# Two feed-forward layers behind a linear attention on one Trainium2 core: the first pass's weight split moves from GpSimd to ScalarE and VectorE, and each chunk's products with low parts come last

## The chip, the cores and the metric

One core of one Trainium2 chip. The metric is the device time of one execution in microseconds; for the kernel before it was measured in three runs. A separate execution was recorded by the hardware profiler and is the source of every row below. Engines are named as in the profile: PE is TensorE (PEld its weight loads), DVE is VectorE, ACT is ScalarE, POOL is GpSimd, SP is SyncE, which here only issues DMAs.

## The reference

```python
def _attn_ref(q, k, v):            # (4, 8, 576, 64) each
    q_s = softmax over the last axis of q
    k_s = softmax over the sequence axis of k
    kv = np.einsum('bhsd,bhse->bhde', k_s, v)
    return np.einsum('bhsd,bhde->bhse', q_s, kv)

x = attn_out.transpose(0, 2, 1, 3).reshape(2304, 512)
h = x @ w_in1; x = (h * sigmoid(h)) @ w_out1         # SiLU,  512 -> 2048 -> 512
h = x @ w_in2; x = (h * tanh(softplus(h))) @ w_out2  # Mish,  512 -> 2048 -> 512
```

The softmaxes subtract the maximum and divide by the sum plus 1e-9. The feed-forward weights reach the chip as 64-bit floating point numbers and are turned into fp32 on the chip; q, k and v are fp32.

## The kernel before, in words

**Layers and passes.** The 2304 tokens are six blocks of 384 (`BLK`, index `j`). Each feed-forward layer is cut into 16 chunks of 128 hidden columns (index `c`) and done in two passes of eight chunks, so that the weights of one pass stay in SBUF: pass 0 and 1 are the SiLU layer, pass 2 and 3 the Mish layer. In a pass, every block goes through eight chunks. `ev_g1` (L645) makes the first products of a chunk (hidden values into a PSUM bank `h`, then SiLU or Mish on ACT into `gf`, then a split of `gf` on DVE), and `ev_g2` (L662) the second products, which add the chunk to the block's four (layer 1) or three (layer 2) accumulators in PSUM; it runs three chunks behind (`SKEW`). `ev_e` (L683) evicts the accumulators. In layer 1 the hidden values have two PSUM banks, so the first product of chunk 5 waits until ACT has read chunk 3.

**Split products.** fp32 operands are split into a high part (fp32r, rounded by a copy) and a low part (the difference), and a product is the sum of three matmuls: high by high, high weight by low activation, low weight by high activation. A chunk has 12 first products (four slices of 128 input features, `kc`, by three parts), and 12 second products in layer 1 or 9 in layer 2. Blocks are split by `ev_x` (L635) on ACT and DVE into `xs`. Weights are split as they arrive: a DMA brings a staging tile `st`; ACT makes `wt` from the upper words (`ACTIVATE wt<-st`), DVE shifts the lower words (`TENSOR_SCALAR st<-st`) and joins the two (`SCALAR_TENSOR_TENSOR wt<-wt,st`). For the 16 weight tiles of pass 0, `w_late` (L168) then lets POOL make the high part (`TENSOR_SCALAR w<-wt`) and the low part (`TENSOR_TENSOR w<-wt,w`). The 48 tiles of the later passes are split by `w_high` and `w_low` (L257, L262), on ACT and DVE.

**Attention under pass 0.** Block 0's attention is written out as a list of steps (`START`, L88); that of blocks 1 to 5 (`attn_steps`) is dealt out between the chunks of pass 0. For a pair of heads (index `hp`, 0 to 3) the steps are: turn k on PE, maximum on DVE, Exp on ACT, turn back on PE, copy by ACT ("ke copy"), 12 products k by v on PE ("kv", rows `psum<-xb,xa 64x64`), scaling on DVE (`kvf`); and for q: maximum on DVE (`qmx`), subtraction on POOL, Exp on ACT, sum on DVE (`qz`), normalisation on POOL (`qn`), turn on PE, copy by ACT (`qT`), product with `kvf` on PE, copy by ACT into the block. Block 1 needs the k of a new batch for all four pairs; its chunks can't start their products with slice `kc` before pair `hp = kc` is done. For block 3 the maximum of k is taken along the free axis (`kmx`, 96x768) without a turn.

**What sets the order.** Every engine runs its queue in order. Until the attention is done, a scheduler sets the order on each engine by priorities; a changed instruction can so move others. After that (`InOrder.on`, from pass 1 on), each engine runs in the order of the program text. SP issues all loads and waits, in its queue's order, until the place a load writes is free.

The nine matmuls of `ev_g1` and `ev_g2` and the two instructions of `w_late` are what the change touches.

Of the kernel before, what the change touches and what calls it, by code (L numbers as in the profile page):

```python
# [7 lines left out]
F32 = mybir.dt.float32  # L8
# [3 lines left out]
ALU = mybir.AluOpType  # L12
# [43 lines left out]
def attention_silu_mish(ctx: ExitStack, tc: tile.TileContext, q, k, v, w_in1, w_out1, w_in2, w_out2, out):  # L56
    nc = tc.nc
    SP = nc.sync
    V, S, G, T = (InOrder(tc, e) for e in (nc.vector, nc.scalar, nc.gpsimd, nc.tensor))
# [4 lines left out]
    P = 128  # L64
    NP = H // 2
    KC = DM // P
# [5 lines left out]
    BLK = 384  # L72
# [42 lines left out]
    def banks(name, ids, n=1):  # L115
        i = turns[name] = (turns.get(name, -1) + 1) % len(ids)
        return psum[:, ids[i] * 512:(ids[i] + n) * 512]
# [50 lines left out]
    def w_late():  # L168
        if state["late"] is None:
            return  # L170
        t, w = state["late"]
        state["late"] = None
        tf = t.bitcast(F32)
        G.tensor_scalar(out=w[:, 0], in0=tf, scalar1=1.0, scalar2=0.0, op0=ALU.mult, op1=ALU.add)
        G.tensor_tensor(out=w[:, 1], in0=tf, in1=w[:, 0].bitcast(F32), op=ALU.subtract)

    def w_decode():

        kind, p, _, c = need[state["dec"]]
        now = tc.cur_priority  # L180
        at(nat[need[state["dec"]]] - W_LEAD)
        state["dec"] += 1
        if not st_q:
            w_dma()
        st = st_q.pop(0).rearrange("p (n t) -> p t n", t=2)
        lo, hi = st[:, 0], st[:, 1]
        t = pools["tm"].tile([P, 512], U32, tag="wt", name="wt")
        V.tensor_scalar(out=lo, in0=lo, scalar1=29, scalar2=None, op0=ALU.logical_shift_right)
        S.activation(out=t.bitcast(F32), in_=hi.bitcast(F32), func=ACTF.Prelu, scale=W_BIAS, alpha=W_SIGN)
        w_late()  # L190
        V.scalar_tensor_tensor(out=t, in0=t, scalar=3, in1=lo, op0=ALU.logical_shift_left, op1=ALU.bitwise_or)
        w = wres.tile([P, 2, 512], F32R, tag="wi" if kind == "G1" else "wo", name="w")
        state["late"] = (t, w)
        w_late()
        wt[(kind, p, c)] = w
        if state["dma"] < N0:
            w_dma()
        tc.cur_priority = now
# [9 lines left out]
    def w_get(kind, p, c):  # L208
        while p == 0 and (kind, p, c) not in wt:
            w_decode()  # L210
        return wt[(kind, p, c)]
# [421 lines left out]
    xs, acc, gt = {}, {}, {}  # L633
# [11 lines left out]
    def ev_g1(p, j, c):  # L645
        L = passes[p][0]
        w = w_get("G1", p, c)
        x = xs[(p, j)]
        h = banks("h1", (4, 5) if L == 0 else (4, 5, 6, 7))[:, :BLK]
        for kc in range(KC):  # L650
            wh, wl = w[:, 0, kc * P:(kc + 1) * P], w[:, 1, kc * P:(kc + 1) * P]
            T.matmul(h, wh, x[:, kc, 0], start=(kc == 0), stop=False)
            T.matmul(h, wh, x[:, kc, 1], start=False, stop=False)
            T.matmul(h, wl, x[:, kc, 0], start=False, stop=(kc == KC - 1))
        g = gr.tile([P, 2, BLK], F32R, tag="g", name="g")
        gf = gp.tile([P, BLK], F32, tag="gf", name="gf")
        S.activation(out=gf, in_=h, func=ACTF.Silu if L == 0 else ACTF.Mish)
        V.tensor_copy(g[:, 0], gf)
        V.tensor_tensor(out=g[:, 1], in0=gf, in1=g[:, 0].bitcast(F32), op=ALU.subtract)
        gt[(p, j, c)] = g  # L660

    def ev_g2(p, j, c, tiles=None):  # L662
        L, c0, c1 = passes[p]
        w = w_get("G2", p, c)
        g = gt[(p, j, c)]
        if c == c0:
            acc[(p, j)] = [banks("acc", (0, 1, 2, 3)) for _ in range(KC if L == 0 else NT2)]
        st, sp = (c == c0), (c == c1 - 1)
        for i, a in enumerate(acc[(p, j)]):
            if tiles is not None and i not in tiles:  # L670
                continue
            s = slice(i * P, (i + 1) * P)
            if L == 0:
                o = a[:, :BLK]
                T.matmul(o, w[:, 0, s], g[:, 0], start=st, stop=False)
                T.matmul(o, w[:, 0, s], g[:, 1], start=False, stop=False)
                T.matmul(o, w[:, 1, s], g[:, 0], start=False, stop=sp)
            else:
                T.matmul(a, g[:, 0, s], w[:, 0], start=st, stop=False)
                T.matmul(a, g[:, 0, s], w[:, 1], start=False, stop=False)  # L680
                T.matmul(a, g[:, 1, s], w[:, 0], start=False, stop=sp)

    def ev_e(p, j, tiles=None):  # L683
        L, c0, c1 = passes[p]
# [25 lines left out]
        out=ident, in_=ident, compare_op=ALU.not_equal, fill=1.0, base=0, pattern=[[-1, P]], channel_multiplier=1  # L710
# [23 lines left out]
    steps = {"first": 0, "rest": 0}  # L734
# [12 lines left out]
    for i, (what, p, j, c) in enumerate(events):  # L747
        if "xs" not in pools and state["dec"] == N0 and not order and i >= xat[1] + PACE[1] * steps["rest"] + A_END:
            w_late()
            l1.close()  # L750
            for nm, nb in (("st", 3), ("tm", W_WAIT), ("xs", 1)):
                pools[nm] = ctx.enter_context(tc.tile_pool(name="l" + nm, bufs=nb, reuse_waits="tile"))
            w_plan(i + 0.5)
            InOrder.on = True
# [15 lines left out]
        if i >= len(events) - SKEW - 2:  # L770
            if what == "G2":
                tail.append(c)
                continue
            for n in range(NT2):
                for c in tail:
                    ev_g2(p, j, c, (n,))
                ev_e(p, j, (n,))
            continue
        if what == "E":
            at(i if InOrder.on else i - X_LEAD)  # L780
            ev_e(p, j)
            continue
        (ev_g1 if what == "G1" else ev_g2)(p, j, c)
        w_ahead(1.0)
        if p == 0 and order:
# [33 lines left out]
```

## Time and profile before

| | |
|---|---|
| median of three runs | 898.5 us (895.59 to 898.77) |
| the profiled execution's own time | 900.18 us |
| its span, first to last instruction | 898.4 us |
| around the span | 1.8 us |
| PE busy | 875.8 us (97%), 5002 matmuls and as many weight loads |
| DVE busy | 452.5 us (50%) |
| ACT busy | 297.3 us (33%) |
| POOL busy | 86.8 us (10%) |
| mean granted TensorE clock | 0.991 |

Busy shares are means over stages that differ. The windows view cuts the span into stretches and gives for each the busy time of every engine, the granted clock and the share of the DMA engines; a stretch with PE below its length, or with the clock below 1.00, is where time can be lost. 1.00 is the higher of the clock's two levels (2.4 GHz), 0.50 the lower (1.2 GHz). Matmuls overlap, so the duration of one is longer than the distance from one to the next.

### The profile page before, as it was taken

The page shows a single profiled execution, that of the slowest core. Times are in us where ns is not written, and L with a number is a line of the kernel's source. Part 1 is how long each engine was busy: PE and PEld are TensorE (multiplying, and loading weights), DVE is VectorE, ACT ScalarE, POOL GpSimd, SP SyncE. Part 2 cuts the span into 40 slices and gives each one's busy share as a digit, 9 for nine tenths or more (in the row PEclk, how much of TensorE's full clock was granted, in tenths as well). Part 3 has the DMA queues.
Part 4 walks back from the last instruction along what each step waited for, and adds up shares of the span by engine and source line. Part 5 has one row for each costly group of instructions (what it writes and reads, how often), then busy time and mean ns, then how long its engine had stood idle before and what let it go on. Part 6 is the DMA issues. An engine that isn't in the chain of part 4 may idle for free.

```text
span 898.4 us, 12437 instructions
## 1 busy us (share of the span) xinstructions
PE 875.8 (97%) x5002; PEld 816.8 (91%) x5002; DVE 452.5 (50%) x949; ACT 297.3 (33%) x576; POOL 86.8 (10%) x114
## 2 busy tenths in 40 slices
PE   7888999999999999999999999999999999999998
PEld 6678888899999999999999998998998998998997
DVE  4997656674257644442348444542349533333332
ACT  5665345554245422121135222222235311211210
POOL 3975302121000000000000000000000000000000
PEclk9998999999999999999999999999999999999999
DMA  9992601220023502200004202200003000000000
GB/s 232 227 242 60 143 13 46 49 62 10 1 94 120 162 24 71 71 24 1 1 1 128 61 24 71 71 24 1 1 1 117 1 36 33 3 36 36 1 36 35
DMA packets 61914, 53.23 MB, mean 59 GB/s; under 512 B 30368, under 2 KB 55456, under 8 KB 61856
## 3 DMA queue, kind: packets, MB, share of 16 engines
q1 hardware_dynamic: 61856, 52.44, 20.7%
q8 instruction: 39, 0.64, 0.3%
q14 instruction: 19, 0.16, 0.1%
HBM read 47.71 MB, written 4.72 MB: 58 GB/s over the span
## 4 chain that ended last, share of the span: by engine, by line
PE 88%; DVE 6%; DMA 2%; SPq 1%; ACT 1%; issue 1%; POOL 0%; ACTq 0%; DVEq 0%; POOLq 0%
PE psum L49 72%; PE psum L47 16%; DVE g L47 1%; DMA st<-in_moe_w_in_dram 1%; DVE wt L47 1%; DVE kmx L47 1%; DVE st L47 1%; SPq L319 1%; DVE xs L47 0%; DMA xb<-in_k_dram 0%; DVE qz L47 0%; DVE qmx L47 0%; ACT xa L47 0%; DMA xa<-in_q_dram 0%; SPq L345 0%
## 5 line engine op out<-in xcount | busy, mean ns | idle before, releaser
L49 PE MATMUL psum<-xs,w 128*128 128x384 f32 x1836 | 335.6, 335 | 1.3 <-DVE xs L49 0.8
L49 PEld LDWEIGHTS psum<-xs,w 128*128 128x128 f32 x1836 | 322.0, 188 | 7.0 <-DVE xs L49 1.1
L49 ACT ACTIVATE gf<-psum 128x384 f32<-128x384 f32 x153 | 75.0, 491 | 405.8 <-PE psum L49 322.3
L49 PE MATMUL psum<-w,g 128*128 128x512 f32 x864 | 208.0, 392 | 0.0
L49 PEld LDWEIGHTS psum<-w,g 128*128 128x128 f32 x864 | 161.3, 188 | 31.0
L49 DVE CAST g<-gf 128x384 fp32r<-128x384 f32 x153 | 55.0, 360 | 253.7 <-ACT gf L49 253.7
L49 PE MATMUL psum<-g,w 128*128 128x384 f32 x720 | 130.6, 334 | 0.0
L49 PEld LDWEIGHTS psum<-g,w 128*128 128x128 f32 x720 | 125.3, 188 | 0.0
L47 PE MATMUL psum<-xs,w 128*128 128x384 f32 x468 | 100.1, 353 | 2.7 <-ACT gf L47 2.3
L49 DVE TENSOR_TENSOR g<-gf,g 128x384 fp32r<-128x384 f32 x153 | 85.4, 558 | 5.3
L47 PE MATMUL psum<-g,w 128*128 128x384 f32 x432 | 87.3, 349 | 0.4 <-DVE g L47 0.4
L47 PEld LDWEIGHTS psum<-xs,w 128*128 128x128 f32 x468 | 81.2, 191 | 6.7 <-POOL w L47 2.3
L47 PEld LDWEIGHTS psum<-g,w 128*128 128x128 f32 x432 | 77.0, 193 | 1.8 <-DVE g L47 0.9
L47 DVE CAST g<-gf 128x384 fp32r<-128x384 f32 x39 | 16.8, 431 | 39.6 <-ACT gf L47 39.4
L49 ACT CAST w<-wt 128x512 fp32r<-128x512 f32 x48 | 29.6, 618 | 21.0 <-DVE wt L49 17.8
L49 DVE TENSOR_TENSOR w<-wt,w 128x512 fp32r<-128x512 f32 x48 | 32.6, 686 | 0.6 <-ACT w L49 0.4
L47 ACT ACTIVATE gf<-psum 128x384 f32<-128x384 f32 x39 | 18.8, 491 | 40.9 <-PE psum L47 35.4
L49 ACT ACTIVATE wt<-st 128x512 f32<-128x512 f32 x48 | 31.8, 672 | 0.0
L47 ACT ACT_TABLE_LOAD x22 | 28.2, 1283 | 3.4 <-PE psum L47 2.3
L49 DVE TENSOR_TENSOR xa<-psum,xa 128x512 f32<-128x512 f32 x18 | 12.3, 692 | 31.9 <-PE psum L49 31.9
L47 DVE TENSOR_TENSOR g<-gf,g 128x384 fp32r<-128x384 f32 x39 | 27.8, 713 | 1.1
L47 ACT COPY xa<-psum 128x384 f32<-128x384 f32 (+2 forms) x36 | 19.4, 538 | 23.4 <-PE psum L47 22.3
(108 smaller groups left out, 588.7 us busy)
## 6 DMA issues: line engine op xcount, KB each, us to landing
st<-in_moe_w_in_dram SPq DMA_DIRECT2D x32, 512.0 KB, 3.9
st<-in_moe_w_out_dram SPq DMA_DIRECT2D x32, 512.0 KB, 3.4
out_dram<-xa SPq DMA_DIRECT2D x18, 256.0 KB, 2.0
xb<-in_k_dram SPq DMA_DIRECT2D x16, 144.0 KB, 3.4
xb<-in_v_dram SPq DMA_DIRECT2D x8, 288.0 KB, 6.6
xa<-in_k_dram SPq DMA_DIRECT2D x16, 144.0 KB, 5.7
xb<-in_v_dram SPq DMA_DIRECT2D x16, 144.0 KB, 3.5
qt<-in_q_dram SPq DMA_DIRECT2D x8, 192.0 KB, 2.7
```

The costliest lines, as they stand in the source:

```text
L47: return call(*args, **kwargs)
L49: self.last = call(*args, **kwargs)
L319: SP.dma_start(kt[:, :, h, :], k[b, 2 * hp + h].rearrange("(p r) d -> p r d", r=KR))
```

## The change

`w_late` puts the high part of a pass 0 weight on ACT and the low part on DVE; POOL has no part in the weights any more. `ev_g1` issues the four slices high by high, then the four with the low activation, then the four with the low weight; the first two chunks of block 0 keep the old order. `ev_g2` does the same over its accumulators, so that each matmul goes to another PSUM bank than the one before, where three in a row went to one.

```diff
@@ w_late
-        G.tensor_scalar(out=w[:, 0], in0=tf, scalar1=1.0, scalar2=0.0, op0=ALU.mult, op1=ALU.add)
-        G.tensor_tensor(out=w[:, 1], in0=tf, in1=w[:, 0].bitcast(F32), op=ALU.subtract)
+        S.copy(w[:, 0], tf)
+        V.tensor_tensor(out=w[:, 1], in0=tf, in1=w[:, 0].bitcast(F32), op=ALU.subtract)
@@ ev_g1
-        for kc in range(KC):
-            wh, wl = w[:, 0, kc * P:(kc + 1) * P], w[:, 1, kc * P:(kc + 1) * P]
-            T.matmul(h, wh, x[:, kc, 0], start=(kc == 0), stop=False)
-            T.matmul(h, wh, x[:, kc, 1], start=False, stop=False)
-            T.matmul(h, wl, x[:, kc, 0], start=False, stop=(kc == KC - 1))
+
+        steps = [(kc, i) for i in range(3) for kc in range(KC)]
+        if (p, j) == (0, 0) and c < 2:
+            steps.sort()
+        for n, (kc, i) in enumerate(steps):
+            s = slice(kc * P, (kc + 1) * P)
+            T.matmul(h, w[:, i // 2, s], x[:, kc, i % 2], start=(n == 0), stop=(n == len(steps) - 1))
@@ ev_g2
-        for i, a in enumerate(acc[(p, j)]):
...
-                T.matmul(o, w[:, 0, s], g[:, 0], start=st, stop=False)
-                T.matmul(o, w[:, 0, s], g[:, 1], start=False, stop=False)
-                T.matmul(o, w[:, 1, s], g[:, 0], start=False, stop=sp)
...
+        for n, (iw, ig) in enumerate(((0, 0), (0, 1), (1, 0))):
+            for i, a in enumerate(acc[(p, j)]):
...
+                if L == 0:
+                    T.matmul(a[:, :BLK], w[:, iw, s], g[:, ig], start=st and n == 0, stop=sp and n == 2)
+                else:
+                    T.matmul(a, g[:, ig, s], w[:, iw], start=st and n == 0, stop=sp and n == 2)
```

The scheduler gives pass 0 another order on every engine up to about the fourth chunk of block 1; behind that PE's instructions stand in the same order as before. Three places follow, the rows before and then the rows of the change.

ACT, block 0: the SiLU of chunk 2 (`gf_518`) to that of chunk 3 (`gf_583`). `xb,kz` is the Exp of a k pair, `xb<-xb` those of q, `xa` the ke copy, `wt` the first step of a weight, ACT_TABLE_LOAD the change between Exp and SiLU.

```order
L47 ACTIVATE gf_518<-psum_78 128x384
L47 ACT_TABLE_LOAD
L47 ACTIVATE xb_77,kz_404<-psum_78,knm_402 128x576
L47 ACTIVATE wt_835<-st_775 128x512
L47 ACT_TABLE_LOAD
L47 ACTIVATE gf_583<-psum_78 128x384
```

```order
L47 ACT_TABLE_LOAD
L47 ACTIVATE xb_77,kz_423<-psum_78,knm_421 128x576
L47 ACTIVATE xb_77<-xb_77 96x256 x3
L47 CAST w_839<-wt_835 128x512
L47 ACTIVATE xb_77<-xb_77 96x256
L47 COPY xa_76<-psum_78 96x768
L47 ACTIVATE wt_869<-st_842 128x512
L47 ACTIVATE wt_904<-st_876 128x512
L47 ACTIVATE wt_957<-st_911 128x512
L47 CAST w_873<-wt_869 128x512
L47 ACT_TABLE_LOAD
L47 ACTIVATE gf_583<-psum_78 128x384
```

Between the SiLU of chunk 0 and that of chunk 3 there now stand six new CASTs (two of them here), three more `wt`, two more table loads, the second k pair's Exp, the four Exps of q and the ke copy, which all came after it before.

SP, the loads behind the last weights of pass 0: `xa<-in_q` is the q of block 2 for one pair (here pair 2), `xa<-in_k` half of the k of block 3 for one pair (here pair 1).

```order
L319 DMA xa<-in_k_dram 96x6x64 x2
L345 DMA xa<-in_q_dram 128x2x192
L345 DMA qt<-in_q_dram 128x2x192
L331 DMA xb<-in_v_dram 96x6x64 x2
L319 DMA xa<-in_k_dram 96x6x64
```

```order
L319 DMA xa<-in_k_dram 96x6x64
L345 DMA xa<-in_q_dram 128x2x192
L319 DMA xa<-in_k_dram 96x6x64
L345 DMA qt<-in_q_dram 128x2x192
L331 DMA xb<-in_v_dram 96x6x64 x2
```

The q load writes where pair 2's k lies until its kv is done; the second half of pair 1's k now stands behind it.

DVE, the end of block 1's attention, up to the scaling `kvf` of pair 3 (`kmx` is the maximum of block 3's k for pairs 0 and 1, `xb<-psum` an eviction of block 0, `xs` a low part of block 1).

```order
L47 TENSOR_REDUCE kmx<-xa 96x128
L47 TENSOR_TENSOR xs<-xa,xs 128x384
L47 COPY xb<-psum 128x384
L47 TENSOR_REDUCE qmx<-xa 128x6
L47 SCALAR_TENSOR_TENSOR kvf<-psum,krz,mask 128x128
```

```order
L47 TENSOR_REDUCE qmx<-xa 128x6
L47 TENSOR_REDUCE kmx<-xa 96x128 x2
L47 TENSOR_REDUCE qz<-xa 128x6 x2
L47 TENSOR_SCALAR qz<-qz 128x6
L47 TENSOR_TENSOR xs<-xa,xs 128x384
L47 COPY xb<-psum 128x384 x2
L47 RECIPROCAL qrz<-qz 128x6
L47 TENSOR_SCALAR qz<-qz 128x6
L47 TENSOR_REDUCE qz<-xa 128x6
L47 SCALAR_TENSOR_TENSOR kvf<-psum,krz,mask 128x128
```

Before, the first of the two `kmx` stood ahead of pair 2's `kvf`; now both stand behind it and behind the `qmx` of pair 2's q, and ahead of pair 3's `kvf`.

## Rows read from the trace of the kernel before

**Rows 1.** Windows; columns: stretch, length, PE, PEld, DVE, ACT, POOL busy, clock, DMA share, GB/s.

```profile
20.00:60.00 40.00, 35.16 (x263) 29.45 (x264) 37.87 (x69) 29.13 (x50) 32.55 (x33) 0.96 0.95 239
60.00:100.00 40.00, 33.26 (x205) 29.80 (x205) 31.89 (x67) 21.92 (x44) 23.72 (x31) 0.83 0.49 111
100.00:898.00 798.00, 791.88 (x4406) 743.78 (x4404) 373.26 (x790) 236.59 (x464) 23.62 (x36) 1.00 0.14 44
```

**Rows 2.** Waits of PE, 30 to 104 us; columns: total us, times, longest.

```profile
PE psum L47 <- DVE kvf L47: 3.3, 1, 3.3
PE psum L47 <- POOL qn L47: 2.7, 1, 2.7
```

**Rows 3.** Windows of 5 us behind these two waits.

```profile
65.00:70.00 5.00, 5.00 (x20) 4.81 (x20) 3.67 (x5) 2.43 (x4) 3.47 (x4) 0.51 0.90 166
85.00:90.00 5.00, 5.00 (x21) 4.62 (x19) 2.56 (x7) 1.99 (x6) 2.81 (x4) 0.50 0.33 69
```

**Rows 4.** DVE's groups, 20 to 100 us; columns: count, busy us, mean ns, idle before.

```profile
L47 DVE SCALAR_TENSOR_TENSOR wt<-wt,st 128x512 uint32<-128x512 uint32 x16 | 16.9, 1054 | 1.3 <-DVE st L47 0.5 <-ACT wt L47 0.3
L47 DVE TENSOR_SCALAR st<-st 128x512 uint32<-128x512 uint32 x15 | 10.7, 716 | 1.2 <-DMA st<-in_moe_w_in_dram 1.2
L47 DVE TENSOR_TENSOR g<-gf,g 128x384 fp32r<-128x384 f32 x8 | 8.7, 1093 | 0.2
...
L47 DVE TENSOR_REDUCE kmx<-xa 96x128 f32<-96x768 f32 x2 | 3.1, 1526 | 0.0
```

**Rows 5.** The same work on DVE, 100 to 898 us, mostly without POOL.

```profile
L49 DVE TENSOR_TENSOR g<-gf,g 128x384 fp32r<-128x384 f32 x153 | 85.4, 558 | 5.3
...
L49 DVE TENSOR_TENSOR w<-wt,w 128x512 fp32r<-128x512 f32 x48 | 32.6, 686 | 0.6 <-ACT w L49 0.4
...
L49 DVE SCALAR_TENSOR_TENSOR wt<-wt,st 128x512 uint32<-128x512 uint32 x31 | 21.3, 686 | 0.6
...
L49 DVE TENSOR_SCALAR st<-st 128x512 uint32<-128x512 uint32 x31 | 13.1, 423 | 0.0
```

**Rows 6.** POOL's weight work in pass 0, 20 to 100 us.

```profile
L47 POOL TENSOR_TENSOR w<-wt,w 128x512 fp32r<-128x512 f32 x16 | 22.8, 1426 | 1.1
L47 POOL TENSOR_SCALAR w<-wt 128x512 fp32r<-128x512 f32 x16 | 12.7, 795 | 10.5 <-DVE wt L47 8.1 <-DVE qz L49 2.5
```

**Rows 7.** The high part on ACT, later passes (costliest groups of the page).

```profile
L49 ACT CAST w<-wt 128x512 fp32r<-128x512 f32 x48 | 29.6, 618 | 21.0 <-DVE wt L49 17.8
```

**Rows 8.** ACT's groups, 20 to 100 us.

```profile
L47 ACT ACT_TABLE_LOAD x9 | 11.5, 1283 | 0.2
L47 ACT ACTIVATE wt<-st 128x512 f32<-128x512 f32 x16 | 10.7, 677 | 5.0 <-POOL w L47 2.6 <-DMA st<-in_moe_w_in_dram 2.3
...
L47 ACT COPY xa<-psum 96x768 f32<-96x768 f32 x4 | 3.1, 788 | 1.0 <-DMA xb<-in_q_dram 0.6 <-PE psum L47 0.3
...
L47 ACT ACTIVATE xb<-xb 96x256 f32<-96x256 f32 x8 | 2.9, 407 | 0.6 <-POOL xb L47 0.6
```

**Rows 9.** ACT's timeline, SiLU of chunks 2 and 3; columns: start, us, what, idle before.

```profile
39.74 0.49 ACT L47 ACTIVATE gf<-psum 128x384 f32<-128x384 f32 x1 [2.17 <-PE psum L47]
...
42.50 0.74 ACT L47 ACTIVATE xb<-psum,knm 128x576 f32<-128x576 f32 x1 [0.96 <-DVE knm L47]
...
45.22 0.49 ACT L47 ACTIVATE gf<-psum 128x384 f32<-128x384 f32 x1
```

**Rows 10.** PE's timeline: the 97th chunk product, pair 1's kv, later chunks.

```profile
53.61 1.72 PE L47 MATMUL psum<-g,w 128*128 128x384 f32 x9
...
58.98 0.92 PE L47 MATMUL psum<-xb,xa 96*64 96x64 f32 x24
...
107.53 2.24 PE L47 MATMUL psum<-g,w 128*128 128x384 f32 x12
109.61 2.24 PE L47 MATMUL psum<-xs,w 128*128 128x384 f32 x12
```

**Rows 11.** Loads of k (L319), 55 to 130 us: landing after issue.

```profile
DMA to landing us min/median/max: 3.3/4.5/6.8
```

More of the change, by code (lines that the diff above doesn't have):

```diff
@@ L668, in ev_g2 @@
         st, sp = (c == c0), (c == c1 - 1)
-        for i, a in enumerate(acc[(p, j)]):
[L670 to L674, printed above, removed]
-                T.matmul(o, w[:, 0, s], g[:, 0], start=st, stop=False)
-                T.matmul(o, w[:, 0, s], g[:, 1], start=False, stop=False)
-                T.matmul(o, w[:, 1, s], g[:, 0], start=False, stop=sp)
[L678 to L681, printed above, removed]
+        for n, (iw, ig) in enumerate(((0, 0), (0, 1), (1, 0))):
+            for i, a in enumerate(acc[(p, j)]):
+                if tiles is not None and i not in tiles:
+                    continue
+                s = slice(i * P, (i + 1) * P)
+                if L == 0:
+                    T.matmul(a[:, :BLK], w[:, iw, s], g[:, ig], start=st and n == 0, stop=sp and n == 2)
+                else:
+                    T.matmul(a, g[:, ig, s], w[:, iw], start=st and n == 0, stop=sp and n == 2)
     def ev_e(p, j, tiles=None):
```

## The prediction

> **What bounds the kernel now.** I read the windows first. From 100 us on PE is busy 791.88 of 798 us at clock 1.00, so that stretch is PE's own work; from 20 to 100 us PE is idle 4.8 and 6.7 us, and the clock is 0.96 and 0.83 [rows 1]. Only this stretch, which is pass 0 on block 0 with the attention of block 1, has time to give. In 20 to 60 us DVE is busy 37.87 of 40 us, ACT 29.13, POOL 32.55 [rows 1]: DVE's queue sets the pace there.
>
> PE's waits come next. Two are long, 3.3 us for DVE's `kvf` of pair 1 and 2.7 us for POOL's `qn` of pair 2 [rows 2], and behind each the clock falls to its lower level, 0.51 and 0.50 in the windows that follow [rows 3]. There PE is busy, but at half rate: 5.00 x 0.49 = 2.45 us and 5.00 x 0.50 = 2.5 us lost. The two waits with their clock cost 3.3 + 2.45 + 2.7 + 2.5 = 10.95 us.
>
> Last the groups, to see why DVE is late. The same DVE instruction takes 1054, 716 and 1093 ns beside POOL, and 686, 423 and 558 ns without it [rows 4, 5]. POOL's weight work and DVE slow each other.
>
> **From 100 us on: nothing, 0.** The number of matmuls and their shapes are unchanged, and PE's queue stands in the same order. The product order is another one, but a run of 12 that stays in one bank and a run that changes bank take the same 2.08 us, from 107.53 to 109.61 us, so 0.174 us a product [rows 10]; evicting four accumulators at the end of a chunk has four chunks of first products as cover. If that cover is gone, each chunk start waits for some evictions; I see no reason for it. A gain made before 100 us is passed on whole.
>
> **DVE and POOL in pass 0.** Removed from POOL: 22.8 + 12.7 = 35.5 us of its 32.55 + 23.72 = 56.3 us between 20 and 100 us, 63% [rows 1, 6]. Relief on DVE, if all slowing goes: 16 x 0.368 = 5.9, 15 x 0.293 = 4.4, 8 x 0.535 = 4.3, in all 14.6 us [rows 4, 5]; if it goes by POOL's share, 63%, 9.2 us. Added to DVE: 16 low parts at 0.686, 11.0 us [rows 5]. Net on DVE between -3.6 and +1.8 us: its sum hardly falls. What changes is that DVE no longer stands still in 1 to 2 us pieces, and that `kvf` and `qz` come sooner in its queue. The Trainium skill, "SBUF — State Buffer", section "Who interferes with whom", says that DVE and GpSimd share a port pair under an exclusive lock, held for a whole instruction, and that a DVE instruction with two SBUF inputs takes part in it; by that the 16 new low parts would hold up POOL's remaining q work in turn, up to 11 us in all, and the waits for `qn` would stay. That is one way into the second rival below.
>
> **ACT in pass 0.** Added: 16 high parts at 0.618 = 9.9 us [rows 7], most of them before 60 us, where ACT has 10.9 us idle [rows 1]. ACT becomes as full as DVE is now. What is queued behind them is the SiLU of chunks. Between those of chunk 0 and chunk 3 the order puts six CASTs (3.7), three `wt` (2.0), two table loads (2.6) [rows 7, 8], one Exp (0.74) [rows 9], four small Exps (half of 2.9) and a copy (0.8) [rows 8] more: 11.3 us. The two waits now there, 2.17 and 0.96 us [rows 9], are covered by the fuller queue. So the SiLU of chunk 3 starts not at 45.22 but at 45.2 + 11.3 - 3.1 = 53.4 us and ends at 53.9. The first product of chunk 5 waits for it. The change has laid 60 first and 36 second products ahead of that; the trace has done 96 by 53.61 us [rows 10]. So PE stands at 53.9 where it stood at 53.6: the lateness is paid for by the second products done earlier. From there the same products and the same attention lead to the end of pair 1's kv, 59.9 us now [rows 10]. **Up to there: 0**, bounds -3.6 (DVE's net) and +8.2 (the whole delay of that SiLU).
>
> **The first wait (kvf of pair 1).** In the changed DVE queue `kvf` stands right behind a low part whose CAST follows the ke copy on ACT; both run while PE makes kv, 0.92 us [rows 10]. `kvf` can then follow kv at once, and PE has three products and two turns as cover. I leave 0.5 us and take away 3.3 + 2.45.
>
> **The second wait (qn of pair 2).** A `kmx` of 1.526 us [rows 4] stood ahead of the `qz` that POOL needs; it now stands after. I leave 0.5 us and take away 2.7 + 2.5.
>
> **A new wait (kvf of pair 3).** SP's order puts half of pair 1's k behind the q load that must wait for pair 2's kv, and DVE's queue holds the `qmx` of that q and both `kmx` ahead of pair 3's `kvf`. After pair 2's kv: landing 4.5 us [rows 11], seven DVE rows of 384 columns at 0.56 (3.9) and two `kmx` (3.05) [rows 4, 5], 11.5 us. PE has meanwhile 32 chunk products at 0.174 (5.6) and some 3.4 us of attention, 9.0. I take +2.5 us. With the landing at 3.3 or 6.8 us [rows 11] it would be 1.3 or 4.8; it is 0 if ACT holds PE up there anyway, and if the clock falls behind it, 2.5 us more.
>
> **Block 1's first chunk.** Slice 3 is now the fourth product of 12, not the tenth, so PE has 13 products less to do while ACT copies and rounds pair 3's part: bounds 0 and 13 x 0.174 = 2.3 us. Two turns and a product of block 2 stand there too; I take +1.0.
>
> **The sum.** -10.95 + 0.5 + 0.5 + 0 + 2.5 + 1.0 = -6.45 us. Against the profiled execution 900.18 - 6.5 = 893.7 us. The median of the three runs, 898.5, lies 1.7 us below it, so I predict 892.0 us.
>
> **Rivals.**
>
> *Slower: ACT takes DVE's place.* ACT's queue is in order, and three `wt` in a row now stand ahead of chunk 3's SiLU, two ahead of the next ke copy; if one of their weights lands late, ACT stands still and PE behind it. Should that hold PE twice for as long as now, 10.95 us, the gain is gone and the rest stays: 0.5 + 0.5 + 2.5 + 1.0 = 4.5 us, 903.0 us. It decides once the SiLU of chunk 3 starts some 3 us after 53.4. For it: DMA share 0.95 in 20 to 60 us [rows 1]. Against it: ACT waited only 2.3 us for weights [rows 8]. Chance 0.14.
>
> *No change: one hold stays.* POOL's q work is still slowed, or DVE is still behind, and one of the two waits with its clock (5.45 us) stays: 892.0 + 5.45, about 897.5 us. For it: DVE's sum hardly falls. Chance 0.21.
>
> *More: PE alone.* All 10.95 us go and DVE's net of 3.6 shows too, with no new wait: 898.5 - 14.6 = 883.9 us. Against it: five engines' queues would have to fit. Chance 0.10.
>
> *The rotation of banks costs clock.* If changing the bank at every second product let the clock fall there, half of the 798 us would take twice as long, some 1,300 us. A run that changes bank every third product shows neither a gap nor a clock below 1.00 today [rows 1, 10]. The Trainium skill, "TensorE: Matmul & The Clock Gate", section "A second HAM failure mode: psum-queue depth-cycling", reports a kernel in which cycling through PSUM banks did make the clock oscillate; this trace does not bear it out at three products a bank. Chance 0.02.
>
> **How the numbers follow.** The forecast has 0.53. 0.5% is 4.5 us, about what a measurement of this kernel can tell from no change. Faster by more than that (below 894.0): the PE case whole, and 0.48 of the forecast's 0.53, 0.58. Slower (above 903.0): half of the ACT case and the banks, rounded up, 0.10. The rest, 0.32. The range runs from 885, a little above the PE case, to 902, which takes in the no-change case and part of the ACT case; some 0.06 lies below it and 0.10 above.
>
> **What would show it.** Right: no `w` rows on POOL; `wt<-wt,st` near 700 to 850 ns in pass 0; 16 more CASTs of about 0.62 us on ACT; no wait of PE for `kvf` of pair 1 or `qn` of pair 2 above 1 us and the clock at 1.00 from 60 to 80 us; a wait for pair 3's `kvf` of 1 to 5 us; the same time per product after block 1. Wrong: a wait of PE for `gf` of chunk 3 or for a ke copy of more than 3 us with a fall of the clock behind it; or any difference that arises after 100 us.

## The result: 8 us faster, and the profile after

The changed kernel took 888.2 us, the median of six executions (887.8 to 892.2); the kernel before, on the same chip, 896.3 us, the median of six (895.6 to 898.8). The ratio is 0.9911, 95% interval 0.9889 to 0.9933: 8.1 us less. The profiled execution took 888.09 us, its span 886.3; that of before, 900.18 us, lies above all six of before's executions here, so the two traces differ by 12.1 us, more than the medians. The section on the prediction comes back to that.

The windows of the changed kernel that answer to [rows 1] and [rows 3], with the same columns:

```profile
20.00:60.00 40.00, 35.01 (x269) 28.95 (x269) 38.29 (x88) 35.21 (x64) 10.73 (x13) 1.00 1.04 255
60.00:100.00 40.00, 38.79 (x265) 35.47 (x266) 31.06 (x72) 24.81 (x50) 15.06 (x20) 1.00 0.66 142
100.00:886.00 786.00, 780.64 (x4339) 732.16 (x4337) 365.60 (x779) 233.00 (x459) 21.34 (x32) 1.00 0.14 42
...
65.00:70.00 5.00, 5.00 (x36) 4.81 (x35) 4.03 (x10) 3.71 (x11) 0.00 (x0) 1.00 0.39 70
85.00:90.00 5.00, 5.00 (x30) 4.86 (x29) 4.85 (x10) 3.67 (x6) 3.58 (x5) 1.00 1.15 239
```

PE does 38.8 us of work in 60 to 100 us where it did 33.3, and all at the full clock. POOL's busy time in 20 to 60 us is a third of what it was, ACT's is up by 6.1 us, and DVE's is as full as before: 38.3 of 40 us. All waits of PE from 30 to 104 us (us in total, times, longest):

```profile
PE psum L47 <- ACT gf L47: 1.9, 2, 1.2
PE psum L47 <- DVE g L47: 1.2, 1, 1.2
PE psum L47 <- ACT qT L47: 0.8, 2, 0.6
PE psum L47 <- DVE kvf L47: 0.7, 1, 0.7
PE psum L47 <- ACT xs L49: 0.3, 1, 0.3
PE psum L47 <- ACT xa L47: 0.3, 1, 0.3
```

The waits for `kvf` of pair 1 and `qn` of pair 2 [rows 2] are gone, and no wait is longer than 1.2 us. DVE's groups from 20 to 100 us, to be read beside [rows 4]:

```profile
L47 DVE SCALAR_TENSOR_TENSOR wt<-wt,st 128x512 uint32<-128x512 uint32 x16 | 11.0, 692 | 0.1
L47 DVE TENSOR_TENSOR w<-wt,w 128x512 fp32r<-128x512 f32 x16 | 10.7, 681 | 0.7 <-ACT w L47 0.6
L47 DVE TENSOR_TENSOR g<-gf,g 128x384 fp32r<-128x384 f32 x13 | 9.2, 710 | 0.3
L47 DVE TENSOR_SCALAR st<-st 128x512 uint32<-128x512 uint32 x15 | 7.0, 475 | 0.4 <-DMA st<-in_moe_w_in_dram 0.4
```

The join of the halves takes 692 ns where it took 1054, the low part of `g` 710 for 1093, the shift 475 for 716. The 16 new low parts fill what this set free. Where the time went is read from PE's timeline. The start of pair 1's kv, of a kv further on and of the last run of pass 3, in the kernel before:

```profile
58.98 0.92 PE L47 MATMUL psum<-xb,xa 96*64 96x64 f32 x24
...
130.66 0.92 PE L47 MATMUL psum<-xb,xa 96*64 96x65 f32 x24
...
886.27 8.36 PE L49 MATMUL psum<-w,g 128*128 128x512 f32 x36
```

and in the changed kernel:

```profile
57.19 0.92 PE L47 MATMUL psum<-xb,xa 96*64 96x64 f32 x24
...
119.03 0.92 PE L47 MATMUL psum<-xb,xa 96*64 96x65 f32 x24
...
874.20 8.36 PE L49 MATMUL psum<-w,g 128*128 128x512 f32 x36
```

The lead is 1.8 us at 58 us, 11.6 us at 131 and 12.1 at 886 (it is 12.1 already at 270, where a run of 12 starts at 270.33 before and at 258.26 after). Most of it, 9.8 us, arises between 59 and 131 us; from there it is carried along but for 0.5 us.

### The profile page after: what moved, and what is told of

Its sections match the earlier page's. It is cut to its first block, busy times and chain, and to the rows that moved or that the text cites. A ratio compares the mean times of both kernels' runs of the same rounds, so it can differ in the third digit from the quotient of the medians.

```text
span 886.3 us, 12434 instructions
## 1 busy us (share of the span) xinstructions
PE 869.8 (98%) x5002; PEld 810.4 (91%) x5002; DVE 444.6 (50%) x965; ACT 303.1 (34%) x592; POOL 54.0 (6%) x82
## 4 chain that ended last, share of the span: by engine, by line
PE 72%; DVE 0%; ACT 0%; issue 0%
PE psum L49 72%; DVE xa L49 0%; ACT xs L49 0%
## 5 line engine op out<-in xcount | busy, mean ns | idle before, releaser
L49 PE MATMUL psum<-g,w 128*128 128x384 f32 x720 | 130.6, 334 | 0.0
L49 PEld LDWEIGHTS psum<-g,w 128*128 128x128 f32 x720 | 125.3, 188 | 0.0
L49 DVE TENSOR_TENSOR g<-gf,g 128x384 fp32r<-128x384 f32 x153 | 85.5, 559 | 5.3
L47 PE MATMUL psum<-g,w 128*128 128x384 f32 x432 | 84.8, 343 | 1.2 <-DVE g L47 1.2
L47 PEld LDWEIGHTS psum<-g,w 128*128 128x128 f32 x432 | 74.7, 188 | 2.6 <-DVE g L47 1.7
L47 DVE CAST g<-gf 128x384 fp32r<-128x384 f32 x39 | 16.3, 419 | 38.8 <-ACT gf L47 38.5
L49 DVE TENSOR_TENSOR xb<-psum,xb 128x384 f32<-128x384 f32 x24 | 11.7, 550 | 30.6 <-PE psum L49 30.6
L47 DVE TENSOR_TENSOR g<-gf,g 128x384 fp32r<-128x384 f32 x39 | 25.0, 641 | 1.0
```

What stands on the lines that cost most here:

```text
L47: return call(*args, **kwargs)
L49: self.last = call(*args, **kwargs)
```

## The experiments

The change has two parts, where the weights are split and the order of the products. My theory was that the first pays, because DVE and POOL hold each other up when they work side by side. The rivals were that the order pays, that what pays is only that POOL's queue is short, or that it is ACT taking over the copies. Every ratio is against the kernel before on the same chip, whose median was 896.9 us (17 executions) for the first four runs, 897.7 (7) for the next three and 897.4 (19) for the last three. A difference from the changed kernel's 888.2 us is one between chips, on which the kernel before lay up to 1.4 us apart; where it matters the ratios are given beside it.

**The split alone (e1_split).** `ev_g1` and `ev_g2` as before, `w_late` as in the change:

```diff
@@ ev_g1, from the changed kernel
-        steps = [(kc, i) for i in range(3) for kc in range(KC)]
...
+        for kc in range(KC):
+            wh, wl = w[:, 0, kc * P:(kc + 1) * P], w[:, 1, kc * P:(kc + 1) * P]
...
```

> Only the weight split moves to ScalarE and VectorE; the products keep their old order (high-high, high-low, low-high slice by slice, three in a row per bank). Theory A (moving the split is what pays): 887 to 890 us, 6.5 to 9 below the kernel before, PE's waits for kvf of pair 1 and qn of pair 2 are below 1 us and the clock stays at 1.00 from 60 to 100 us. Theory B (putting the low parts last is what pays, because PE no longer waits for them): 896 to 900 us, with new waits of PE for the low parts that VectorE now makes, 3 us or more in all between 30 and 60 us.

Measured 888.6 us (888.0 to 891.2), ratio 0.9909 [0.9895, 0.9924]: the whole gain. Its longest waits of PE are those of the changed kernel, 1.4 us and less.

**The order alone (e2_order).** The new order of products, the weights on POOL as before:

```diff
@@ w_late, from the changed kernel
-        S.copy(w[:, 0], tf)
-        V.tensor_tensor(out=w[:, 1], in0=tf, in1=w[:, 0].bitcast(F32), op=ALU.subtract)
+        G.tensor_scalar(out=w[:, 0], in0=tf, scalar1=1.0, scalar2=0.0, op0=ALU.mult, op1=ALU.add)
+        G.tensor_tensor(out=w[:, 1], in0=tf, in1=w[:, 0].bitcast(F32), op=ALU.subtract)
```

> Only the products change their order; GpSimd keeps splitting pass 0's weights. Theory A: 895 to 897 us, within 1.5 us of the kernel before; VectorE's join of weights still takes about 1050 ns on average in pass 0 and PE still waits 2 us or more for kvf of pair 1 or for qn of pair 2. Theory B: 887 to 890 us.

Measured 896.4 us (894.7 to 898.2, 12 executions), ratio 0.9992 [0.9981, 1.0003]: no difference that can be told. PE's waits, 30 to 104 us:

```profile
PE psum L47 <- DVE kvf L47: 3.4, 1, 3.4
PE psum L47 <- POOL qn L47: 2.7, 1, 2.7
```

The two waits of [rows 2] stand there to a tenth. The order of the products is not what removed them. The join took 924 ns, not the 1050 that I had expected; the shift took 866 for 716 in [rows 4], so the two together are as slow as before, 1790 and 1770 ns.

**The split and the new first products, the old second products (e3_g2old).** `ev_g2` as before, the rest as changed:

```diff
@@ ev_g2, from the changed kernel
-        for n, (iw, ig) in enumerate(((0, 0), (0, 1), (1, 0))):
-            for i, a in enumerate(acc[(p, j)]):
...
+        for i, a in enumerate(acc[(p, j)]):
...
```

> The whole change, but the second products go three in a row to one PSUM bank as before. If the order of the second products matters neither way (my view): 888 us within 1.5 us of the whole change. If going through the banks one by one costs clock or time after 100 us: faster than the whole change by more than 2 us. If second products with the low part last are what keeps PE from waiting for VectorE: 891 us or more, with waits of PE for g of 2 us or more in pass 0.

Measured 889.5 us (887.5 to 892.2), ratio 0.9919 [0.9903, 0.9935]; its interval overlaps that of the changed kernel. The order of the second products, and with it the change of bank at every matmul, is worth nothing that these runs can tell. The profiled execution, 892.2 us, was the longest of the six; in it PE waits up to 2.2 us for `gf` and 1.9 for `g`, and the clock is at 0.66 in 55 to 60 us.

**POOL works on, for nothing (e4_dummy).** The changed kernel, and POOL in addition does its two old instructions for each late weight, into a tile that nothing reads:

```diff
@@ w_late, from the changed kernel
         V.tensor_tensor(out=w[:, 1], in0=tf, in1=w[:, 0].bitcast(F32), op=ALU.subtract)
+        G.tensor_scalar(out=busy[0], in0=w[:, 0].bitcast(F32), scalar1=1.0, scalar2=0.0, op0=ALU.mult, op1=ALU.add)
+        G.tensor_tensor(out=busy[0], in0=busy[0], in1=w[:, 0].bitcast(F32), op=ALU.subtract)
```

> The whole change, and GpSimd does the same two instructions per weight once more into a scratch tile that nothing reads (the computation itself is complete). Theory A1 (GpSimd and VectorE slow each other by running at once): VectorE's join is back at 900 to 1050 ns in pass 0, and 4 us or more of the gain are lost: 892 us or more. Theory A2 (only the weights' wait in GpSimd's queue mattered): the join stays near 700 to 750 ns or, if it is slow, the time still stays at 888 to 890 us.

Measured 908.1 us (906.2 to 909.0), ratio 1.0115 [1.0099, 1.0131]: 19.9 us above the changed kernel's 888.2 (18.3 by the ratios), and 11.1 us slower than the kernel before. DVE's and POOL's groups, 20 to 100 us:

```profile
L47 DVE TENSOR_TENSOR w<-wt,w 128x512 fp32r<-128x512 f32 x16 | 18.0, 1146 | 0.0
L47 DVE SCALAR_TENSOR_TENSOR wt<-wt,st 128x512 uint32<-128x512 uint32 x16 | 16.4, 1029 | 0.0
...
L47 DVE TENSOR_REDUCE qz<-xb 96x4 f32<-96x256 f32 x8 | 3.1, 402 | 0.0
```

```profile
L47 POOL TENSOR_TENSOR busy<-busy,w 128x512 f32<-128x512 f32 x16 | 23.2, 1448 | 1.0
L47 POOL TENSOR_SCALAR busy<-w 128x512 f32<-128x512 f32 x16 | 15.7, 984 | 7.1 <-ACT w L47 6.7
L47 POOL TENSOR_TENSOR qn<-xb,qrz 96x256 f32<-96x256 f32 x8 | 10.1, 1268 | 6.2 <-DVE qz L47 3.4 <-DVE qrz L47 2.8
```

and POOL's `qn` in the kernel before:

```profile
L47 POOL TENSOR_TENSOR qn<-xb,qrz 96x256 f32<-96x256 f32 x8 | 6.2, 785 | 3.1 <-DVE qz L47 3.1
```

Nobody reads what POOL makes there, and yet DVE's join goes from 692 back to 1029 ns, its low part from 681 to 1146, and POOL's `qn` from 785 ns before to 1268. DVE's reductions of one tile stay at 402 ns. PE waits 6.3 us for `qn` and 6.0 for `gf` between 30 and 104 us, and in 60 to 100 us the clock is 0.83 again. One reserve: POOL's extra instructions also let the scheduler set another order than in the changed kernel, so not all of the 19.9 us need be mutual slowing; e8 and e9 below bear on that.

**Half of it back on POOL (e5_lowpool, e6_highpool).** In e5 the low part goes back to POOL, in e6 the high part:

```diff
@@ w_late, e5_lowpool, from the changed kernel
-        V.tensor_tensor(out=w[:, 1], in0=tf, in1=w[:, 0].bitcast(F32), op=ALU.subtract)
+        G.tensor_tensor(out=w[:, 1], in0=tf, in1=w[:, 0].bitcast(F32), op=ALU.subtract)
@@ w_late, e6_highpool, from the changed kernel
-        S.copy(w[:, 0], tf)
+        G.tensor_scalar(out=w[:, 0], in0=tf, scalar1=1.0, scalar2=0.0, op0=ALU.mult, op1=ALU.add)
```

> The changed kernel with the low part of the late weights alone back on POOL (the high part stays on ACT, the new product order stays). POOL's 16 subtractions of two tiles were 22.8 of its 35.5 us of weight work. If what pays is that an instruction of two tiles no longer runs on POOL beside DVE's, most of the loss comes back: 894 us or more, the DVE join of the halves (w, from t and st) again above 850 ns, and a wait of PE above 2 us for kvf or for POOL's qn. If what paid was that ACT takes the copies, or that POOL's queue became short, the time stays at 888 to 890, with the join near 700 ns.

> The changed kernel with the high part of the late weights alone back on POOL (the low part stays on DVE). POOL's 16 copies of one tile were 12.7 us, so 0.8 us each; a low part on DVE must now wait for POOL's queue. If only subtractions of two tiles on POOL get in DVE's way, the time stays at 888 to 891 and the join near 700 ns. If any work on POOL does, some 36% of the loss comes back (12.7 of 35.5 us): 891 to 893. If low parts that stand in DVE's queue behind POOL's late copies hold DVE up, it is 896 or more, with PE waits for kvf or gf above 3 us.

Measured 893.0 us for e5 (892.1 to 893.5), ratio 0.9944 [0.9929, 0.9958], and 892.4 for e6 (891.1 to 893.4), ratio 0.9933 [0.9916, 0.995]. They lie 4.8 and 4.2 us above the changed kernel, and 4.9 and 4.3 above e7 (888.1 us, below), which ran on their chip; by the ratios it is only 3.0 and 2.0 us, and e6's interval reaches into the changed kernel's. So each half costs between a quarter and six tenths of the gain. In e5 the join takes 788 ns, less than the 850 that I had expected, and no wait for `kvf` or `qn` reaches 2 us; its longest is 2.0 us, for the ke copy on ACT, and its loss of clock lies early (0.66 in 35 to 40 us). DVE is slowed there all the same, in rows that I had not named: the shift takes 680 ns for 475, the low part of `g` 847 for 710. In e6 the join is untouched, but DVE's low part is not:

```profile
L47 DVE TENSOR_TENSOR w<-wt,w 128x512 fp32r<-128x512 f32 x16 | 13.0, 820 | 2.3 <-POOL w L47 2.2
L47 DVE SCALAR_TENSOR_TENSOR wt<-wt,st 128x512 uint32<-128x512 uint32 x16 | 11.0, 696 | 0.9 <-ACT wt L47 0.8
```

The share by POOL's time (36%, 891 to 893) fits e6. But there DVE also waits 2.2 us for POOL's `w`, and PE 1.1, so e6 alone does not tell a slowed DVE from one that waits for POOL's queue; the next pair does.

**Only a subtraction, only a copy (e8_dummysub, e9_dummycopy).** These two repeat e4 with one of its two instructions, so that the results again pass through ACT and DVE alone:

```diff
@@ w_late, e8_dummysub, from the changed kernel
+        G.tensor_tensor(out=busy[0], in0=tf, in1=w[:, 0].bitcast(F32), op=ALU.subtract)
@@ w_late, e9_dummycopy, from the changed kernel
+        G.tensor_scalar(out=busy[0], in0=w[:, 0].bitcast(F32), scalar1=1.0, scalar2=0.0, op0=ALU.mult, op1=ALU.add)
```

> The changed kernel with one more instruction of POOL per late weight: the subtraction of two tiles that was there before, its result put into a tile that nothing reads. DVE and ACT do their work as in the change. If what hurts is an instruction of two tiles on POOL beside DVE's (16 of 1.4 us, 23 of the 39 us that POOL did in the run with both instructions, which cost 20 us), most of those 20 us come from it: 900 us or more, the join of the halves on DVE above 900 ns. If any work of POOL hurts alike, 12 us: 900. If POOL's queue was the trouble, POOL's qn is waited for again, 2 us or more each time, with the join below 800 ns.

> The same with POOL's copy of one tile in place of the subtraction, its result read by nothing. If only instructions of two tiles on POOL stretch DVE's, the time is 888 to 890 and the join of the halves near 700 ns. If any work of POOL hurts alike, 16 of 39 us of POOL's work give 8 of 20 us: 896.

Measured 904.9 us for the subtraction (901.6 to 905.7), ratio 1.0077 [1.0055, 1.01], and 894.6 for the copy (892.1 to 897.4, ten executions), ratio 0.997 [0.9954, 0.9987]: 16.7 and 6.4 us above the changed kernel's 888.2 (14.9 and 5.3 by the ratios). DVE's and POOL's groups with the subtraction:

```profile
L47 DVE TENSOR_TENSOR w<-wt,w 128x512 fp32r<-128x512 f32 x16 | 16.1, 1023 | 0.0
L47 DVE SCALAR_TENSOR_TENSOR wt<-wt,st 128x512 uint32<-128x512 uint32 x16 | 12.3, 776 | 1.2 <-ACT wt L47 1.2
...
L47 POOL TENSOR_TENSOR busy<-wt,w 128x512 f32<-128x512 f32 x16 | 24.6, 1538 | 12.4 <-ACT w L47 9.6 <-DMA xb<-in_v_dram 2.5
```

and with the copy:

```profile
L47 DVE TENSOR_TENSOR w<-wt,w 128x512 fp32r<-128x512 f32 x16 | 13.6, 871 | 0.5 <-ACT w L47 0.5
L47 DVE SCALAR_TENSOR_TENSOR wt<-wt,st 128x512 uint32<-128x512 uint32 x16 | 11.2, 706 | 0.0
...
L47 POOL TENSOR_SCALAR busy<-w 128x512 f32<-128x512 f32 x16 | 20.0, 1251 | 10.5 <-ACT w L47 10.1
```

I had expected 888 to 890 for the copy if only two-tile work on POOL hurts, and 896 if all of it does alike. It lies between, so the claim that only a subtraction on POOL hurts falls: 0.68 us lost per us of POOL's work for the subtraction (16.7 / 24.6), 0.32 for the copy (6.4 / 20.0). What is stretched beside either is above all the low part, 1023 and 871 ns for 681; the join, which I had taken as the mark, moves less (776 and 706 for 692). With the copy PE's longest wait, 2.3 us, is for POOL's `qn`, and the clock of 0.68 in the window of 60 to 65 us goes with it; this profile, 892.1 us, was the shortest of its ten executions. With the subtraction PE waits 0.3 us for `qn`, but 7.7 for `gf` and 2.6 for `kvf`: there the work of ACT and DVE is late, not POOL's.

The means hide how the slowing comes about. The tile views of the run with the copy give minimum, median and maximum in ns:

```profile
L47 DVE TENSOR_TENSOR w<-wt,w x16: 672/680/1715, 22.8 to 74.9; 128x512 fp32r<-128x512 f32 x16
L47 POOL TENSOR_SCALAR busy<-w x16: 612/920/4270, 22.5 to 75.0; 128x512 f32<-128x512 f32 x16
```

At least half of DVE's low parts take 680 ns or less, as without POOL's work; a few take up to 1715. One copy on POOL stood for 4.27 us, from 51.09, while DVE went through a row of instructions of which none took 0.7 us. So it is single instructions that are held up for long, on either engine, and the `qn` that PE waits for stands behind such copies in POOL's queue.

The order that the scheduler set does not explain the differences within this group. From 20 to about 100 us the rows of DVE and of ACT stand in the same order in e4, e8 and e9, but for one or two records that a trace lacks; e8 and e9 ran on one chip, and with nothing but POOL's instruction different they lie 10.3 us apart. Of e9's own 6.4 us a part can still be the order. Nor is it ACT taking over the copies that pays: in e4 and e8 ACT has them and the whole gain is gone, in e5 a third of it or more.

**Low parts of the weights two events later on DVE (e7_later2000).** An attempt to beat the change, by letting DVE reach the low part of `g`, for which PE waited 1.2 us, sooner:

```diff
@@ w_late, from the changed kernel
         S.copy(w[:, 0], tf)
+        now = tc.cur_priority
+        tc.cur_priority = now + 2000
         V.tensor_tensor(out=w[:, 1], in0=tf, in1=w[:, 0].bitcast(F32), op=ALU.subtract)
+        tc.cur_priority = now
```

> The changed kernel in which the low part of a late weight is put two events later in DVE's order, so that the low part of g, on which PE waited 1.2 us in pass 0, comes sooner. Nothing else is changed. If that wait is DVE's queue standing on low parts of weights, it goes: 887.0 us, 0.1% below the change, and hardly to be told from it. If the weights become the late ones instead, PE waits for w and the time is 889 to 892.

Measured 888.1 us (887.6 to 890.1), ratio 0.9894 [0.988, 0.9909]: not to be told from the change. The wait for `g` shrinks to 0.8 us; waits for `qT` (1.7 in all) and for k (1.1) take its place.

**The kernel before, again (e10_before).** No edit.

> The kernel before, unchanged, profiled a second time. Its first profile had the clock at 0.66 in 25 to 30 us, a fall that the prediction did not count, and lay above the median of its runs. If that fall belongs to the kernel, it is there again, and the change took it away. If it comes and goes from one execution to the next, this profile has 1.00 there, a time of 896 to 897 us, and the two waits for kvf and qn as before, each with its fall.

Measured 898.2 us (896.2 to 899.9), ratio 1.0007 [0.9995, 1.0019]; the profiled execution took 899.9 us. Windows of 20 to 25, 25 to 30 and behind the two waits:

```profile
20.00:25.00 5.00, 4.54 (x49) 3.26 (x51) 4.42 (x11) 4.67 (x10) 3.10 (x4) 0.70 0.83 281
25.00:30.00 5.00, 5.00 (x28) 3.84 (x25) 4.81 (x6) 2.16 (x5) 4.83 (x5) 0.62 0.67 215
65.00:70.00 5.00, 5.00 (x20) 4.81 (x19) 3.77 (x6) 2.81 (x5) 3.06 (x4) 0.52 1.10 166
85.00:90.00 5.00, 5.00 (x20) 4.63 (x19) 2.50 (x6) 1.87 (x5) 2.53 (x4) 0.50 0.21 45
```

The falls behind the two waits repeat to a hundredth. The early one is there again, and larger, so the two profiles don't tell whether it comes with every execution: both were long ones, and over these ten the mean clock goes from 0.998 (896.2 us) to 0.989 (899.9 us). Why one execution takes it and another not stays open. The groups vary too: the same join and shift, 1054 and 716 ns in [rows 4], are here

```profile
L47 DVE SCALAR_TENSOR_TENSOR wt<-wt,st 128x512 uint32<-128x512 uint32 x16 | 14.6, 912 | 1.2 <-ACT gf L47 0.5 <-ACT wt L47 0.3
L47 DVE TENSOR_SCALAR st<-st 128x512 uint32<-128x512 uint32 x15 | 13.0, 864 | 0.0
```

with nearly the same sum (1776 and 1770). What the early fall costs can be read from the order alone (e2), which ran at 1.00 there:

```profile
25.00:30.00 5.00, 2.76 (x11) 1.58 (x10) 4.90 (x6) 3.81 (x7) 4.83 (x5) 1.00 0.77 226
```

```profile
30.22 0.91 PE L49 MATMUL psum<-xa,kvf 128*128 128x384 f32 x2 [1.99 <-DVE xs L49]
...
32.93 2.02 PE L47 MATMUL psum<-xs,w 128*128 128x384 f32 x10 [0.40 <-DVE xs L49]
```

At the full clock PE was busy only 2.76 of those 5 us, waited 1.99 us for DVE's `xs`, and came to the rest of block 0's first chunks no sooner than the kernel before did with the fall. Up to there the lower clock only fills time in which PE would wait for DVE.

## Why the prediction was right

It said 892.0 us, 885 to 902, with faster by over 0.5% as the likeliest; it came to 888.2, 0.9% faster. The mechanism held. POOL has no weight rows, `wt<-wt,st` is at 692 ns, just under the 700 to 850 foreseen, 16 new CASTs of 0.62 us stand on ACT, both waits are gone and the clock is 1.00 from 20 us on. The terms held less well than the total. Step by step, between the two traces:

- **From 100 us on, 0.** Right within 0.5 us: the lead at 131 us, where the two orders stand alike again, is 11.6 us and at the end 12.1. The 0.5 us arise where pass 1 begins: PE waited there for a block's split (`xs`), 0.46 and 0.82 us, and now 0.83 once. That is the new order's doing, which the sum put at nothing: e1 still has both waits, e2 the one. The runs of 12 that change bank at every matmul still follow each other every 2.08 us, at clock 1.00:

```profile
92.67 2.24 PE L47 MATMUL psum<-g,w 128*128 128x384 f32 x12
94.75 2.24 PE L47 MATMUL psum<-xs,w 128*128 128x384 f32 x12
```

  With the ratio of the order alone, 0.9992, the rival of the banks is out. The Trainium skill, "TensorE: Matmul & The Clock Gate", section "A second HAM failure mode: psum-queue depth-cycling", tells of a kernel that cycles through PSUM banks, in which PE idles between groups and the clock oscillates; here one product a bank brings neither the idle time nor the lower clock.
- **DVE and POOL in pass 0.** Right in kind, and nearer the full end than POOL's share: join, shift and `g` went from 1054 to 692, 716 to 475 and 1093 to 710 ns, which on the counts of [rows 4] is 5.8 + 3.6 + 3.1 = 12.5 us of the 14.6, where the share gave 9.2. DVE's sum did not fall: 38.3 of 40 us for 37.9.
- **Up to pair 1's kv, 0.** This step failed, by 1.8 us between these two traces (0.4 us between those of e2 and e1), inside its bounds (-3.6 to +8.2). The relief of DVE came to PE at a place that the sum does not name, block 0's `xs`, the low parts of which DVE makes between the weights. The run of block 0's first chunks in the changed kernel starts 2.4 us before its counterpart (32.35 us):

```profile
29.94 2.73 PE L47 MATMUL psum<-xs,w 128*128 128x384 f32 x12 [0.30 <-ACT xs L49]
```

  The split alone has that run at 29.23 us, the order alone the last ten of it at 32.93: it is the split. PE's waits don't show it in the trace of before, since the clock is 0.66 in that window and PE is busy all through it:

```profile
25.00:30.00 5.00, 5.00 (x29) 3.60 (x25) 4.81 (x6) 2.92 (x6) 4.83 (x5) 0.66 0.69 210
```

  The SiLU of chunk 3, forecast to end at 53.9 us, ended at 51.8, and the first product of chunk 5 follows:

```profile
51.86 1.66 PE L47 MATMUL psum<-xs,w 128*128 128x384 f32 x8 [0.72 <-ACT gf L47]
```

  That this product, which stands where the 97th stood at 53.61, waits for ACT was right, and so was the balance of a fuller ACT and earlier second products: of the 2.4 us of lead 1.8 are left there.
- **The two waits.** Right for the trace that they were read from: both waits and both falls are gone. From pair 1's kv to the later kv the lead grows by 11.6 - 1.8 = 9.8 us; the sum had 6.45 for this stretch. But the price of the falls was that of a long execution: over the 6 us behind each wait they took 5.6 us there, and 3.2 us in e2, whose profile (896.3 us) lies at the median (rows in the last section).
- **A new wait (kvf of pair 3).** Right in its place, wrong in size: 0.7 us, not 2.5, with no fall of the clock.

```profile
82.40 0.59 PE L47 MATMUL psum<-qT,kvf 128*128 128x192 f32 x2 [0.72 <-DVE kvf L47]
```

- **Block 1's first chunk.** Wrong: +1.0 forecast, but PE does not wait for block 1's split (`xs`) at all, and goes into its first run of 24 without any wait, where before it had waited 0.65 us for `gf`:

```profile
88.40 4.43 PE L47 MATMUL psum<-xs,w 128*128 128x384 f32 x24
```

  These two terms account for 2.8 of the 3.4 us that the stretch is better than the sum.
- **The step from profile to median.** I took 1.7 us off for the median. The two profiled executions of before (900.18 and 899.9) are among its longest; beside the change its median was 896.3. So the traces differ by 12.1 us and the medians by 8.1. The forecast lands 3.8 us too high: 2.2 from that median, 1.6 from a gain of 8.1 instead of 6.5. That the gain came so near is partly luck: against the trace that it was added up from, 6.45 is 5.6 us short; for a usual execution the falls were priced 2.4 us too high, and the 3.5 us of new waits, of which 0.7 came, made up for it.

Of the rivals, "ACT takes DVE's place" did not come: ACT's work grew to 35.2 of 40 us, and the longest wait of PE for `gf` is 1.2 us, with no fall behind it. "One hold stays" did not come. Beside DVE's new low parts POOL's `qn` took 920 ns instead of 785, but PE did not wait for it. That is the direction in which the lock works that the Trainium skill describes ("SBUF — State Buffer", section "Who interferes with whom"), but it is far from making the waits for `qn` stay. The same section of the Trainium skill lets a DVE instruction with two SBUF inputs contend with GpSimd's reads and a reduction never; e4, with 1146 and 402 ns for the two, agrees.

## What to carry to other kernels

When two engines hold each other up, the engine that is off the path is dear: a us of POOL's work whose result nobody reads cost 0.3 to 0.7 us of the whole kernel here, so price moved work by what it does to the neighbour's rows, by reading the same instruction with and without the neighbour. A busy sum that does not fall (DVE, 37.9 to 38.3 of 40 us) says little: what went was the lateness of two instructions on which PE stood still long enough to lose its clock as well. And a stretch in which PE is busy throughout at a lowered clock can hide a wait: the same stretch at the full clock showed PE waiting 2 us for the engine that the change then freed.

## What the runs showed of the chip that I had not expected

A one-tile copy on POOL is not harmless beside DVE: in e9 DVE's two-tile low part took 871 ns on the mean for 681, and the POOL copy itself 1251 ns, where it took 795 in the kernel before [rows 6]. The stretching thus goes both ways, by a few long holds, and it falls on different rows of DVE in different runs (the join in e4, hardly in e9; join or shift in two executions of the kernel before), so one row alone, or its mean, is a poor gauge of it. A wait of the same length does not always bring the same loss of clock. Behind waits of 3.3 and 2.7 us, which ended at 64.65 and 84.17 us, the kernel before ran the next 6 us at 0.57 and 0.50:

```profile
64.65:70.65 6.00, 6.00 (x23) 5.81 (x24) 4.67 (x7) 2.94 (x5) 3.97 (x5) 0.57 0.85 153
84.17:90.17 6.00, 6.00 (x23) 5.62 (x24) 3.56 (x9) 2.19 (x6) 3.59 (x6) 0.50 0.34 73
```

Behind waits of 3.4 and 2.7 us, which ended at 63.85 and 82.48 us, the order alone (e2) ran them at 0.75 and 0.72:

```profile
63.85:69.85 6.00, 6.00 (x29) 5.70 (x30) 4.93 (x9) 3.26 (x6) 4.54 (x6) 0.75 0.90 188
82.48:88.48 6.00, 6.00 (x28) 5.21 (x28) 4.08 (x10) 2.62 (x7) 4.08 (x8) 0.72 0.33 73
```

That is 2.58 + 3.00 = 5.6 us lost against 1.50 + 1.68 = 3.2, 2.4 of the 3.9 us by which the two profiled executions differ. Whether the product order or the execution makes the difference these traces do not tell.
